# A new order, new engines and new buffer slots for a planned one-core kernel, and single loads in place of split ones

## The chip, the cores and the metric

The kernel runs on one core of a Trainium2 chip. The metric is the device time of one execution in microseconds (us), the median of several runs. The engines are called as in the profile: PE (TensorE, matmuls; PEld are its weight loads), DVE (VectorE), ACT (ScalarE), POOL (GpSimd) and SP (SyncE, which here issues every DMA).

## The reference

Gated linear attention with a state for each of 4 batches and 8 heads, and behind it a token mixer of low rank and an MLP, whose output is added:

```python
q, k, v, alpha: (4, 8, 768, 48) float32
for t in range(S):
    state = alpha[:, :, t, :, None] * state + einsum('bhd,bhe->bhde', k[:, :, t], v[:, :, t])
    y[:, :, t] = einsum('bhd,bhde->bhe', q[:, :, t], state)
x  = y as (4, 768, 384)
u  = x + (x.transpose(0, 2, 1) @ U @ V).transpose(0, 2, 1)      # U (768, 32), V (32, 768)
out = u + maximum(u @ w_ch1, 0) @ w_ch2                          # (384, 1536), (1536, 384)
```

## The kernel before, in words

The work of each batch goes through five stages. **Attention** works on units of a batch, written b.u here (0.4 is batch 0, unit 4). In batches 0 and 1 and the first two units of batch 2 a unit is half of the heads over two chunks of 64 pairs of tokens (`stage_pair`); the other units are one chunk of 128 tokens with all heads (`stage_gla`). A unit loads alpha, k, q and v (192 KB each, tiles `io`), takes the logarithm of alpha on ACT (tile `lt`, L390), sums it along the tokens on PE (L399 to L406), takes exponentials on ACT (tiles `ai`, `aa`, `tot`), multiplies k and q by them on POOL or DVE (tile `rkq`, L421), transposes the two products on PE (L449) and copies them out of PSUM on ACT or DVE (tile `kqt`, L294 or L296). Scores are matmuls of 64x64 tiles in pair units (L480) and of 64-row tiles in the others (L658); DVE masks them (L491, L668). The state's update is 64-row matmuls (L514) and, in batch 0, an identity matmul that adds the state before (L506), which must wait for DVE's state product (L529); in batch 1 DVE adds it instead (tile `sm`, L543). The output is full matmuls with the state (L562) and 64-row ones with the masked scores (L572), copied to `xb`.

**Mix** (`stage_mix`) multiplies x by U (L750) and by V (L771), DVE adds the two into `ub` (L781, eight quarters), and u is transposed on PE (L819) in batches 0 and 1, by DMA transposes on SP (L805) in batches 2 and 3. Batch 3's k and q are transposed by DMA too (L642). **MLP 1** (`mlp1`) has 24 groups for each batch of three matmuls (L851), each evicted with a relu by ACT (L861) or DVE (L863). **MLP 2** (`mlp2`) has three groups of four matmuls (L880) for each of 6 chunks, then DVE adds u (L886) and SP stores (L889, L891). The last chunk of the last batch is made in two column parts (240 and 144).

Nothing of the order is left to the compiler. `Plan.add` collects 1065 operations in the order of the program with the buffers that each reads and writes. `Plan.run` then emits them in the order of the string `TABLE`: three characters for each, of which the first two are the operation's number in base 64 and the third its engine (P, A, D, G for POOL, S). `SLOTS` has a character for each of the 736 buffers, at the place where a buffer is first used: which slot of its pool (`io` has 40, PSUM 8 banks) it takes. Each engine works its own operations in this order, waiting for what they need. The costs in the `P.add` calls are those of the search outside the kernel that made the strings. A field `mode` marks the shape of the PE tiles: F full, H and R 64 rows, Q 64x64, and three shapes of the mixer with 32 rows or columns.

Loads of pair units are always one transfer. Loads of other units go through L359 to L367: for eight of them `SPLIT` names a row at which the 128 rows are divided between two transfers, issued one after the other.

## Time and profile before

| | |
|---|---|
| time, median of 3 runs | 159.99 us (159.78 to 160.29) |
| the profiled execution | 159.3 us, span 157.5 us |
| granted TensorE clock in the clock column | 1.000 |
| DMA | 31.68 MB, mean 201 GB/s |
| first PE matmul, first MLP-1 group, last PE matmul | start 3.97, start 30.84, end 154.58 us |

The span is the time from the first to the last instruction; the profiled execution takes 1.8 us more than that. PE's matmuls are pipelined, so their lengths overlap, and the time that a group costs is read from its start to the start of the next one. A wait is given as waiting engine, what it was about to do, the releaser, and then the total in us, how often, and the longest.

### The profile page before, as it was taken

Reading aid. Unit: us, or ns where it says so; the run is one execution under the profiler, and the core shown is the slowest. Engines: PE = TensorE matmul, PEld = TensorE weight load, DVE = VectorE, ACT = ScalarE, POOL = GpSimd, SP = SyncE. Lnnn points to the kernel's source line nnn. Section 1 sums busy time; section 2 is a strip of 40 time slices with the busy share of each in tenths; the row PEclk is TensorE's granted clock in tenths of the full one; section 3 lists DMA queues with packets and bytes.
Section 4 is the critical chain, followed back from the end, with each engine's and each line's share of the span. In section 5 each row is a group of like instructions: output and inputs, shape, how many; then the busy total and the mean of one; then the engine's idle time right before and its main releaser. Section 6 shows DMA issues by size and latency. Waiting matters only on the chain.

```text
span 157.5 us, 4982 instructions
## 1 busy us (share of the span) xinstructions
PE 147.0 (93%) x1940; PEld 98.8 (63%) x1940; DVE 111.0 (70%) x253; ACT 85.7 (54%) x223; POOL 62.6 (40%) x103
## 2 busy tenths in 40 slices
PE   0499999889999999999999999999999999999992
PEld 0387676656687757666666765666667565666572
DVE  5168899956999636668899979399889634462351
ACT  4487998759897565499296740344552301532000
POOL 8155867635999704524375640055531000000000
PEclk9999999999999999999999999999999999999999
DMA  5999998999999979999989792899885062367475
GB/s 130 273 272 320 280 232 232 299 314 332 331 325 284 273 153 244 190 218 201 197 170 227 145 200 51 138 201 162 165 176 126 0 104 52 126 154 219 138 216 175
DMA packets 91275, 31.68 MB, mean 201 GB/s; under 512 B 84948, under 2 KB 91220, under 8 KB 91252
## 3 DMA queue, kind: packets, MB, share of 16 engines
q1 hardware_dynamic: 91252, 31.37, 83.4%
q8 instruction: 15, 0.25, 0.7%
q14 instruction: 8, 0.07, 0.1%
HBM read 23.89 MB, written 4.72 MB: 182 GB/s over the span
## 4 chain that ended last, share of the span: by engine, by line
PE 76%; SPq 17%; DMA 3%; issue 1%; DVE 1%; DVEq 0%
PE ps L880 31%; PE ps L851 29%; SPq L353 13%; DMA io<-in_k_dram 3%; PE ps L449 2%; SPq L326 2%; PE ps L658 2%; PE ps L572 1%; PE ps L480 1%; PE ps L725 1%; PE ps L630 1%; SPq L301 1%; PE ps L720 1%; PE ps L595 1%; PE ps L771 1%
## 5 line engine op out<-in xcount | busy, mean ns | idle before, releaser
L851 PE MATMUL ps<-uT,w_sb 128*128 128x384 bf16 x288 | 53.3, 326 | 0.7 <-DVE sm L543 0.4
L880 PE MATMUL ps<-w_sb,h1t 128*128 128x384 bf16 (+2 forms) x300 | 53.3, 320 | 0.0
L861 ACT ACTIVATE h1t<-ps 128x384 bf16<-128x384 f32 x54 | 25.3, 497 | 29.9 <-PE ps L851 28.0
L851 PEld LDWEIGHTS <-w_sb 128*128 128x128 bf16 x288 | 26.8, 98 | 16.9 <-issue 1.0
L880 PEld LDWEIGHTS <-h1t 128*128 128x128 bf16 x300 | 26.9, 98 | 15.4
L863 DVE TENSOR_SCALAR h1t<-ps 128x384 bf16<-128x384 f32 x42 | 22.2, 552 | 11.7 <-PE ps L851 11.6
L886 DVE TENSOR_TENSOR io<-ub,ps 128x384 f32<-128x384 bf16 (+2 forms) x25 | 13.1, 534 | 9.1 <-PE ps L880 8.8
L491 DVE TENSOR_TENSOR pm<-ps,maskp 128x512 bf16<-128x512 f32 x28 | 18.1, 682 | 0.1
L781 DVE TENSOR_TENSOR ub<-xb,ps 128x288 bf16<-128x288 bf16 x32 | 12.3, 448 | 4.9 <-ACT lt L390 3.1
L294 ACT COPY kqt<-ps 128x512 bf16<-128x512 bf16 x24 | 13.8, 592 | 3.2 <-PE ps L630 2.4
L668 DVE TENSOR_TENSOR pm<-ps,maskc 128x512 bf16<-128x512 f32 x20 | 12.7, 683 | 1.1 <-PE ps L658 1.1
L421 POOL TENSOR_TENSOR rkq<-io,aa 128x384 bf16<-128x384 f32 x12 | 10.9, 911 | 5.2 <-DMA io<-in_q_dram 4.2
L294 ACT CAST xb<-ps 128x192 bf16<-128x192 f32 (+1 forms) x24 | 8.1, 369 | 8.9 <-PE ps L725 6.5
L449 PE MATMUL ps<-ident,rkq 128*128 128x128 bf16 x112 | 11.1, 236 | 2.0 <-DVE rkq L421 1.5
L616 POOL TENSOR_TENSOR rkq<-io,aa 128x384 bf16<-128x384 f32 x9 | 8.5, 949 | 11.2 <-DVE io L886 8.0
L421 POOL TENSOR_TENSOR rkq<-io,ai 128x384 bf16<-128x384 f32 x8 | 8.1, 1015 | 11.6 <-ACT ai L413 11.6
L298 POOL CAST rv<-io 128x384 bf16<-128x384 f32 x19 | 10.0, 530 | 5.4 <-DMA io<-in_v_dram 4.8
L298 POOL CAST w_sb<-io 128x384 bf16<-128x384 f32 x17 | 8.2, 506 | 5.1 <-DMA io<-in_moe_w_ch_dram 5.1
L449 PEld LDWEIGHTS <-rkq 128*128 128x128 bf16 x112 | 7.7, 104 | 4.0 <-DVE rkq L421 1.7
L399 PE MATMUL ps<-lt,upto 128*128 128x384 bf16 x14 | 5.4, 385 | 4.8 <-ACT lt L390 4.8
L616 POOL TENSOR_TENSOR rkq<-io,ai 128x384 bf16<-128x384 f32 x5 | 4.6, 915 | 9.8 <-DMA io<-in_k_dram 5.0
L390 ACT ACTIVATE lt<-io 128x384 bf16<-128x384 f32 x14 | 7.2, 533 | 2.2 <-DMA io<-in_alpha_dram 2.2
(108 smaller groups left out, 208.7 us busy)
## 6 DMA issues: line engine op xcount, KB each, us to landing
...
```

Source lines behind the costliest of these rows:

```text
L294: nc.scalar.copy(dst, src)
L298: nc.gpsimd.tensor_copy(dst, src)
L353: lambda e: nc.sync.dma_start(t().rearrange("p (h j) d -> p h (j d)", j=2), src[b, hs, sl, :].rearrange("h (p j) d -> p h (j d)", j=2)),
L421: eng.tensor_tensor(jh(dst()[:, :, 0:D]), raw(a), jh(x()), op=ALU.mult)
L449: nc.tensor.matmul(dst, lhsT=ring()[:, HP * j + 2 * a : HP * j + 2 * a + 2, :].rearrange("t h w -> t (h w)"), rhs=ident, start=True, stop= ...
L491: nc.vector.tensor_tensor(dst, s2, maskp.to_broadcast([C, 2, 2, C]), op=ALU.mult)
L616: eng.tensor_tensor(dst()[:, :, 0:D], a(), x(), op=ALU.mult)
L851: nc.tensor.matmul(hb()[:, 0:TW], lhsT=w1_sb[:, ct, jt * 128 : (jt + 1) * 128], rhs=u_half(uT, ct, tt, b in QUEUE_U), start=(ct == 0), sto ...
L861: nc.scalar.activation(dst, hb()[:, 0:TW], AF.Relu)
L863: nc.vector.tensor_scalar_max(dst, hb()[:, 0:TW], 0.0)
L880: nc.tensor.matmul(hb()[:, 0 : hi - lo], lhsT=h1()[:, jt, c * C : (c + 1) * C], rhs=w2_sb[:, jt, lo:hi], start=(jt == 0 and not low), stop ...
L886: P.add({"DVE": 468}, lambda e, hb=hb, lo=lo, hi=hi: nc.vector.tensor_tensor(flat(ou)[:, lo:hi], (xb if low else ub)()[:, c, lo:hi], hb()[ ...
```

## The change

The two strings are replaced throughout; `Plan.run`, the operations and their matmuls stay. Decoded, the strings say this:

- Operations by engine: DVE 230 before and 233 after, ACT 222 and 227, POOL 88 and 80, PE 351 and SP 174 in both. Of the 96 MLP-1 evictions ACT has 54 before and 61 after, DVE 42 and 35. Of the 24 weight casts POOL has 17 before and 14 after, ACT 7 and 10.
- Neighbours on PE with a 64-row group next to a 64x64 group: 5 before, 8 after. All neighbours of unlike shape (H and R as one): 77 before, 76 after.
- PE's first seven groups and SP's first eight loads are the same. Then SP has v of 0.1 ahead of q of 0.1. PE's groups 8 to 15 were q transposes 0.1, state update 0.1, state update 0.0, k transposes 0.0, identity 0.1, identity 0.0, scores 0.1, scores 0.2; now they are state update 0.1, q transposes 0.1, identity 0.1, scores 0.2, state update 0.0, identity 0.0, k transposes 0.0, scores 0.1.
- The two small matmuls that spread V over the partitions stand behind batch 0's last output group before, and both ahead of it after; their copies (`ve_sb`) were one on DVE behind batch 0 and one on ACT, and are now one on DVE amid batch 0 and one on ACT. DVE's list between batch 0's last mask and the first `ub` sum was a state product, three `xb` copies, a `ve_sb` copy and a k copy; now it is one `xb` copy, a q copy and the mixer's small copy.
- Batch 0's MLP 1 began with groups mixed with the sums and transposes of 1.3, 1.1 and 1.2 (their k and q transposes came after 2 to 14 groups); now thirteen groups run before the transposes of 1.1. k of 1.1 was SP's 42nd operation and is now its 46th; its product with `ai` moves from DVE to POOL.
- In batch 3 the six DMA transposes of k and q have the order 2, 0, 1, 3, 4, 5 before and 0, 2, 1, 3, 4, 5 after. The loads of k and q of 3.4 stand behind batch 2's three DMA transposes of u in both; the scores of 3.4 come sooner after them on PE: they were the last but one of that batch's six and are now the fourth.
- PE's last groups were one of batch 3's chunk 4 and then five part-groups of chunk 3; now they are one of chunk 4 and two part-groups of chunk 3.

The diff, with the strings cut to their first and last lines:

```diff
 TABLE = """
-BASCzAC1PC4ABESDKADMPDPABISDOAC2ABBSBGSDRDDTPDjAA8SCcACePBFSC5GC7PDlPC3ADNADQDDSPC9DChAA9SCfACiDDVDBCSBDSC0AC6GC8PC+DDnA
...
-PQiDQjSQWPQaPQXPQYDQZSQbPQcPQdDQeS
+BASCzAC1PC4ABESDKADMPDPABISDOAC2ABBSBGSDRDDTPDjAA8SCcACePBFSC5GC7PDlPC3ADNADQDDSPC9DChAA9SCfABDSC0ABCSDoADnAA-
...
+PQlPQmPPnDPpDPdAQYDPtDQQPQaPQGPQRPQfPQLPQHPQnDQgPQIPQJDQMPQSPQTDQNPQhPQoSQKSNRSQODQUSQPSQiDQjSQZSQbPQcPQdDQeS
 """
 SLOTS = """
-AAAABBBBCAADEACCFADGBEFBBGACHCCBIJAHCAABAKBECLMNDBAOBDFACPCQDHAAEBGBBRBCSDCFTBUVDAWHCGAADXYZabDcdFECAADCDCeABEAGfgChijkl
...
-AGEDPHEQDJFBUcAd
+AAAABABBCAADEACAFBDABEFABBACGABAHDBIBAGJEEDFABACCAHIAGABHBABJAEBCKEFAHBBCGBCDFGABCFEBCAAHDLMNDCAAHBGJIGAAEBABBFDCAOPFQRS
...
+HFCDAQADGCEIXGIJ
 """
...
     PAIRS = {0: 3, 1: 3, 2: 1, 3: 0}
-    kn, qn, vn = (x.tensor.name for x in (k, q, v))
-    SPLIT = {
-        (2, 5, qn): 117, (2, 4, kn): 108, (3, 2, vn): 110, (3, 1, kn): 126,
-        (3, 2, qn): 117, (3, 0, qn): 108, (3, 0, kn): 110, (3, 3, kn): 126,
-    }
     QUEUE_T = tuple((3, c) for c in range(6))
...
-            at = SPLIT.get((b, c, src.tensor.name), C)
-            P.add(
-                {"SP": 1100.0},
-                lambda e: [
-                    nc.sync.dma_start(t()[lo:hi], src[b, :, c * C + lo : c * C + hi, :].rearrange("h t d -> t h d"))
-                    for lo, hi in ((0, at), (at, C)) if lo < hi
-                ],
-                w=[t],
-            )
+            sl = slice(c * C, (c + 1) * C)
+            P.add({"SP": 1100.0}, lambda e: nc.sync.dma_start(t(), src[b, :, sl, :].rearrange("h t d -> t h d")), w=[t])
```

More of the change, by code (lines that the diff above doesn't have):

```diff
@@ new lines @@
+SDUAC6DDCPA+SC8PBQSBMSBJSBHSCdGDDDDVACiDDEPDWPBKSDFDC+DBRSABSCgABLSDmACrPCsDDYDCtPCkPCuDCjGBSSETABNSBUSBOSBTSC-PDGPDZPD8
+ADBDDADCmAClPDpGDLGEVPCnAD+PDrPBPSEWAEYADXDBWSDaPCoPDtDDqGEXABYSAASBcSBkSAFGBVSBXSDHPDbDDkGEZGDcPDfPEaGDdDCpDDyPBgSAQSAM
+SDJADsPDePCqDEAAD-AEBADzPDgPAJPDuADiAD0DAKDDvPAOSDhADIAAgSD1PEcPD2DAiSAeSAWSAUSEeAASSBaSBdSEbPEiPBZSBeSBbSBfSDxDAaSECGCv
+PELPEEPGQAEGAEdDEDGEfPDwDEFPEHAGSPBmSAYSEUGEhDEgDBlSAcSD9GBhSGUACwPCxAEjPCyABoSGXGEMPEIPEkDEJDD3PBiSENDElPD4PEmPEnPEpAGT
+AEoAD5PGVABjSBqSEOPAkSADGGWGALGEPPEKDAoSAmSD6AD7AAGPEQPESDAqSERAGRGGZPGbDAHAEqPErDGnAHwAG+AEsPEwDExPGpPE1DEtDGYPHAPGrAGa
@@ new lines @@
+AHDAGsABpSARGEuDEvDE0DHyPEzDGfPANGAhGHXAE2PEyDGgDH1AE4PBnSHZPE6PGhDE3AAPABrSGcPAfGE5DGqAHzAATGGiDFAPAuSFBAAwSAySAsSA2SA0
+SHBAE7DA6SA4SAjAHCAGdDFUPE8PFVDGeDE9AE+PBzSFWPFYPFSPFQPFOPE-
+DAXAGuDGtGBsSHcAAVAFTAFXAFCPBxSBwSHEDFcPFePFDDHFDGoGFZAHbAHaAFdAFaPGwPFRDFmPG-GGvPFbAH0AHGPHHPFnAHIDFGPGyDGxAFoPAbGH3GHJ
+DFPDFfAAZGFHAAdGG2PHNPFpAHODGzPHdGB0SB4SBtSCASG3DG0DG4DHKPFEPFqPFFAIHACGSBuSBySFiPHPGH2DFjAFrAFgPIJPFhAG1DHLDHfPH5PH4PFI
+PHYAIKAHMDHeGG5GH7DILACBSB6SHQDIMAFJAGjPHgPFkPH6DHSPAlGHTPFlAHhDHiDHmPHUPGkPHVAHnDHWAB8SGlAH8PIOGHoDHjPAnAApAArGINGHpDIQ
@@ new lines @@
+PFKPFMPFLAISAGmAH9DGKPHrPCFSHkDHxGH+DHlDHsPCSSB1SIPPIRDFNAG6PG7PHRDHtPIIAG8AH-
+PIWPHuAIADITPHqGHvAIXDICPG9DIUDF+PF4PIVDIYGAvGIBGFsPB2SB3SAxGIDPAtAAzAIaPA3AA5AIZPIbPIcDKbAIEPGLPIFDA7GA1GIdDIGDF-PIePB-
+SB7SFtPIfDIgPGAPIjDGMPBvSIiDIkDFuPGBDF5PIhDIlPKEAFyPF6PIoDImDKdPKGPKJAKyAInDIpDKfAKHAF7DIsPGEPFvDIuPKIAGFPGGPFzPB9SItDLI
+AKKDKeALyAKLDCESB5SIvAACSB+SCQSKgAKiGGNDL0PIqPKkPF0PKhGKNPKmDIrDKjPL2AFwSGHDF1DKPDJKPKcGK0PK3AKlAI2PJQPL1AJWPKnPK1AK2ALK
+PLNAK4AL3GJLDLOAK6GI3DJMPCMSCDSCCSCTSK5GCYSGCSKoDCPSJNDJaPJYPJIPLMALLAJXAJbAK8PJcPKMPJJAJdAI6PJZDLeGK7PKOAI0PIwPKFGJRAKp
@@ new lines @@
+DK9AIxAK+DCLSKTPK-
+PI7DI1DKqPLJGLQGLdAKzGKUDKQPJSPLADCNSCISKSDJTAKrDKsDI4PJUPJVACXSCHSLfPJGPJOPLCPI5ANhAKVDLBDKtDLPDLhALEDI+PKWGI-ALDDLlDKR
+DNjPJCPJHALRPJEPLFGLTDJAPJPDJePLSPNnANkALgALiAJfDJFDLYPLkDJBAJDALjALUAI8PLZDKuPLGPI9AKvPLHAKxDKwAOWALVPLmPLWDL5PLnPKXPJ4
+PL4GL7DLtPLpAL6PLaGLoAIyPJ5PAEGAIGLXDLqPNmALzGOEALuDKYPCOSL8DIzANlACbSCUSCaSNyAL9PLvGL-
+DLrDJmPJnPJoPOGPLbPLsDKaDLcAN0PL+DLwPJ6POIAMAPCJSJ+PKZDLxDMBANzAN3AMCPOoAOJAOHAOKAJpDJ7DMDDJ-
+PCKSMEPJsPKAPMIDMHDMGDMJPO6AMFDMMDMNDNoGNiGNpGNqSCZSCRSJtPMOSJgPOpGOXAOFAN2AN1AN4AMKDOYPO8PNuPKBDOcAOZAMLDObAMPSJyPN5GN-
@@ new lines @@
+PNvDOLDO+AOMDONSOADJhPJzPOqPMQSCVSOtAOuAOaAORPJuPCWSOBGN6GJ0PJiPMbPMZPJ1DMdPOSDOrAOsAMcDJvDN7SMaAMeANrPOOPOQDNtDOdDJjDMT
+PNsDMVPMRPM1POeGMWAO9AM2DOPDM3POvGMvPMhPMUDGOSMwDOTDNwPJxSMSANxAOfSOwGMfPOUPOVDOjPMnPMoAMXPMpPM5PMiDOkDM4DMrPOxSMqAMYAMz
+PN8PMsDN+DOyPJ8SF9SM6AO0DN9DOgPGJSOzDM0APAGO-GMgAM-PNAAOlGM9PMtPO1PMjPO2DM+DOiDO3GGDSJkSPBSGPSF8SM7POCPO4PMxPMkAOhDMlPPC
+PMyDJ3SF2SO7AODAOmPPDDNHPO5ANBPPEDOnAMuAPFPNSPPGAMmAPHPNTPPIDM8DPJPNIPNJPJwSPKDPNDPMDNXPPLDPOPNYPPQDPRDPTSNNPNOPPPDNcPNd
+PF3SPSDNCPNZPNUPPUSNDPNePPWPPVSFxSNfDNEDNVDNKDNaDPuPPcPNPPJlSPkPPlDPgPPhAPYPP+PNQDQCPNGSJ9SGISP2PJ2SPwPQDAPvDP6PP7DPxAPX
```

37 lines of the change are left out of this document (6 added, 31 removed).

## The prediction

> **What bounds the kernel now.** I read the page's busy line, then the busy time by stretches of 4 us (columns: stretch, its length, then busy us of PE, weight loads, DVE, ACT, POOL; granted clock, DMA share, GB/s), and then who waits for whom, for PE alone.
>
> ```profile
> PE 147.0 (93%) x1940; PEld 98.8 (63%) x1940; DVE 111.0 (70%) x253; ACT 85.7 (54%) x223; POOL 62.6 (40%) x103
> ```
>
> ```profile
> 4.00:8.00 4.00, 1.86 (x17) 1.34 (x17) 0.68 (x3) 2.04 (x7) 0.48 (x2) 1.00 1.04 274
> ...
> 16.00:20.00 4.00, 3.58 (x87) 2.71 (x86) 3.29 (x9) 3.72 (x10) 3.58 (x5) 1.00 1.06 277
> 20.00:24.00 4.00, 4.00 (x108) 3.10 (x105) 4.00 (x9) 3.80 (x11) 2.55 (x5) 1.00 0.84 214
> 24.00:28.00 4.00, 3.75 (x109) 2.69 (x106) 3.66 (x11) 3.27 (x10) 2.42 (x4) 1.00 0.96 258
> 28.00:32.00 4.00, 3.59 (x63) 2.81 (x64) 3.65 (x9) 3.14 (x7) 2.89 (x6) 1.00 1.01 290
> 32.00:36.00 4.00, 3.57 (x27) 2.13 (x26) 2.60 (x7) 2.28 (x8) 1.10 (x3) 1.00 1.05 322
> 36.00:40.00 4.00, 4.00 (x32) 2.52 (x30) 2.81 (x6) 3.44 (x10) 2.70 (x6) 1.00 1.09 335
> ...
> 148.00:152.00 4.00, 4.00 (x28) 2.54 (x26) 1.95 (x4) 0.00 (x0) 0.00 (x0) 1.00 0.63 161
> ```
>
> ```profile
> PE ps L399 <- ACT lt L390: 4.8, 3, 4.0
> ...
> PE ps L851 <- DVE sm L543: 0.4, 1, 0.4
> ```
>
> From 36 to 152 us all 29 rows (the first and the last are shown) have PE at 4.00 of 4.00: nothing can be saved there except PE's own work. What a new order can win lies before 36 us, where PE idles (the 4.8 us are mostly the wait for the first load) and where DVE is nearly full too (4.00 at 20 to 24), and in the last 3 us. The PE timeline says how (columns: start, length with the modelled end, line, count, idle before it):
>
> ```profile
> 7.94 0.61 PE L449 MATMUL ps<-ident,rkq 128*128 128x128 bf16 x4 [1.47 <-DVE rkq L421]
> ...
> 10.10 0.37 PE L401 MATMUL ps<-lt,upto 128*128 128x192 bf16 x1
> 10.26 0.21 PE L402 MATMUL ps<-offd,ident 128*128 128x8 bf16 x1
> ...
> 14.29 0.25 PE L400 MATMUL ps<-lt,below 128*128 128x192 bf16 x1
> 14.38 0.25 PE L401 MATMUL ps<-lt,upto 128*128 128x192 bf16 x1
> ...
> 14.90 0.34 PE L514 MATMUL ps<-rv,rkq 64*128 64x96 bf16 x8
> 15.08 0.36 PE L572 MATMUL ps<-rv,pm 64*128 64x48 bf16 x16
> ...
> 17.77 0.34 PE L514 MATMUL ps<-rv,rkq 64*128 64x96 bf16 x8
> 18.04 0.80 PE L480 MATMUL ps<-kqt 48*64 48x128 bf16 x32
> ...
> 24.71 0.37 PE L572 MATMUL ps<-rv,pm 64*128 64x48 bf16 x16
> ...
> 30.84 0.65 PE L851 MATMUL ps<-uT,w_sb 128*128 128x384 bf16 x3 [0.26 <-DVE uT L296]
> ...
> 32.48 1.81 PE L851 MATMUL ps<-uT,w_sb 128*128 128x384 bf16 x9
> 34.70 0.65 PE L851 MATMUL ps<-uT,w_sb 128*128 128x384 bf16 x3 [0.40 <-DVE sm L543]
> ...
> 130.99 7.48 PE L851 MATMUL ps<-uT,w_sb 128*128 128x384 bf16 x45
> 138.30 0.81 PE L880 MATMUL ps<-w_sb,h1t 128*128 128x384 bf16 x4
> ```
>
> Steps are read from start to start. A 192-column matmul takes 0.16 us at 10.10 and 0.09 at 14.29: PE runs at half pace until 14.29, though the clock column says 1.00 in every row. An MLP-1 group (three matmuls) takes (138.30 - 130.99) / 15 = 0.487 us, so the three groups from 32.48 to 34.70 lost 2.22 - 1.46 = 0.76 us. The first MLP-1 group starts at 30.84; from there the kernel is PE's list plus those 0.76 us and little else.
>
> **The change part by part.** Each of the 351 PE groups runs in both tables with the same matmuls.
>
> *Changes of tile shape.* Eight 64-row matmuls (L514) take 15.08 - 14.90 = 0.18 us where 64-row work follows, and 18.04 - 17.77 = 0.27 where 64x64 work does: a change costs about 0.09, and a few ns more behind it. Adjacent groups of 64-row and of 64x64 tiles meet 5 times in the old order and 8 times in the new one, so the new charge has not made them fewer; the new order instead groups those stages, away from full tiles. All changes of shape together are 77 before and 76 after. That is one change: -0.1 us.
>
> *The start, to the first MLP-1 group.* Here I follow DVE, the fuller partner, in both orders.
>
> ```profile
> 13.75 1.89 DVE L491 TENSOR_TENSOR pm<-ps,maskp 128x512 bf16<-128x512 f32 x3
> ...
> 22.91 1.29 DVE L491 TENSOR_TENSOR pm<-ps,maskp 128x512 bf16<-128x512 f32 x2
> 24.12 0.35 DVE L529 TENSOR_TENSOR st<-ps,tot 128x192 bf16<-128x192 f32 x1
> 24.54 1.01 DVE L296 CAST xb<-ps 128x192 bf16<-128x192 f32 x3
> 25.46 0.55 DVE L296 CAST ve_sb<-ps 128x384 bf16<-128x384 f32 x1
> ...
> 26.64 3.01 DVE L781 TENSOR_TENSOR ub<-xb,ps 128x288 bf16<-128x288 bf16 x8
> ...
> 33.82 0.56 DVE L421 TENSOR_TENSOR rkq<-io,ai 128x384 bf16<-128x384 f32 x1 [0.71 <-DMA io<-in_k_dram]
> 34.30 0.35 DVE L543 TENSOR_TENSOR sm<-ps,st 128x192 f32<-128x192 f32 x1
> ```
>
> The first eight loads and PE's first seven groups are the same. The new DVE list has about 0.8 us more work ahead of batch 0's last mask (a ve copy of 0.46 and one more 0.33 copy), but its first mask can go at about 13.3 instead of 13.75, and its order leaves fewer holes behind; stepping through it with the row durations (mask 0.60, state 0.27, copies 0.33) I get the last mask done at 24.2, as now. Behind it the new order has less: the old DVE list has a state product, three xb casts and a ve copy there before the first u sum at 26.64; the new one has the state product and one ve copy ahead of the mask, gives xb casts to ACT, and on PE both ve matmuls stand ahead of the last output group instead of behind it. That last group can start just behind the mask, at 24.3 instead of 24.71, and the same 1.93 us (26.64 - 24.71) behind it the first u sum goes at about 26.3. Eight sums at 0.365 and a state product with its sum (0.53, in place of a mask of 0.60) later, DVE copies the transposed u at about 29.9. PE still has a score group to run first, so its first MLP-1 group starts at about 30.85, as before, but with 0.23 us more of its list done: adding up the steps of the groups ahead of it gives 18.86 us in the new order and 18.63 in the old. So: -0.2 us. The bounds are wide, since each step waits on another engine: -0.8 if every hole of 14 to 30 us that I count closes, +0.5 if two holes like the 0.51 and 0.70 us that DVE now has before its L529 products come back.
>
> *The start of the MLP.* The 0.76 us were lost because DVE's queue stood behind the k tile of batch 1, unit 1 (0.71 us for the DMA), and a PSUM bank waited behind it. The new order runs thirteen MLP-1 groups, 13 x 0.487 = 6.3 us, before it needs that tile, gives the product to POOL, and loads w1 blocks in the order of use. DVE still has a product on a q tile there. I take -0.45, between 0 and -0.76.
>
> *From 36 us on.* Seven more MLP-1 evictions go to ACT, POOL loses eight operations; both lie beside PE. If a cover goes, a late eviction costs PE its own length, some 0.5 us; I take 0, with 0 to +0.3.
>
> *The loads.* A split load costs two issues on SP.
>
> ```profile
> 77.28 1.20 SPq L363 DMA_DIRECT2D io<-in_v_dram  x2
> ...
> 81.22 0.67 SPq L363 DMA_DIRECT2D io<-in_v_dram  x1
> ```
>
> Eight of them at 1.20 - 0.67 = 0.53 us free about 4 us of SP between 74 and 91 us. PE waits for nothing there, so this is worth 0; what comes earlier behind it are loads of batch 3, and their buffers set when they may start.
>
> *The end.*
>
> ```profile
> 153.13 2.22 SPq L891 DMA_DIRECT2D out_dram<-io  x4
> 154.12 0.41 DVE L886 TENSOR_TENSOR io<-ub,ps 128x240 f32<-128x240 bf16 x1 [0.52 <-PE ps L880]
> 154.69 0.30 DVE L886 TENSOR_TENSOR io<-ub,ps 128x144 f32<-128x144 bf16 x1 [0.17 <-PE ps L880]
> ```
>
> Now chunk 4 is finished five part-groups before the end and the last store leaves right behind the last sum. In the new order chunk 4's last group stands directly before the last two, so three sums and three stores come within about 1 us, and the last sum waits for the one before it: +0.2 us (0 to +0.3).
>
> Sum: -0.1 - 0.2 - 0.45 + 0 + 0 + 0.2 = -0.55 us. The profiled execution took 159.3 us with a span of 157.5; the span becomes about 156.95 and that execution 158.75. The median of the three runs shown, 159.99, lies 0.69 above the profiled one, so the median becomes 159.4. About 0.3% (0.48 us) is what a measurement of this kernel can tell from no change, so this stands just past that line, at 159.5.
>
> **The rivals.** *No change that can be measured, 159.9.* The start is a ring of PE, ACT, DVE and POOL; each row of 16 to 32 us has two of them above 3.5 of 4. If a hole closed on one engine opens on another, the start gains 0 and the MLP's start 0.2: -0.1 - 0.2 + 0.2 = -0.1. For it: DVE is at 4.00 in 20 to 24 and has more work ahead of the last mask. Against it: the work behind that mask is less.
>
> *The clock comes later, 161.3.* The half pace ended at 14.29, 6.35 us after the last gap of note (1.47 us before 7.94). Behind its first L514 group the old PE order has another such group and a transposition before the identity product (L506) that needs DVE's state; the new one has one transposition there and then 64x64 scores that need two copies from ACT, and so should idle about 1 us in pieces between 11.5 and 13.5. If that restarts whatever the 6.35 us were, half pace lasts to 19.8, 5.5 us more, in which PE does up to 2.75 us less; some 0.9 us of that falls into holes that it has anyway from 14 to 20 us: +1.85 on the forecast. It decides if the first full-pace step lies after 15 us. Against it: the pieces are short, none as long as the gap of 1.47.
> [...]
>
> *A late tile in batch 3, 160.8.* k and q of batch 3, unit 4 are issued on SP behind three transposes that wait for batch 2's u sums, and their own transpose behind two stores and two more transposes. By SP's steps it lands about 1.6 us before PE's turn. A slip above that stops PE for about what it slips; I price it at 1.4.
>
> *The change does not do what it says.* The count of changes (5 to 8) is such a case already; it is inside the forecast.
>
> **How the numbers follow.** Forecast 0.50 (its own range 158.5 to 159.5), no change 0.28, later clock 0.15, late tile 0.07. Faster by over 0.3% is the forecast, 0.50; within it, the second case, 0.28; slower, the other two, 0.22. The range starts at 158.5, where the start gains 0.8 and the MLP's start all of its 0.76 against +0.2 at the end, a little short of the sum of all the best ends (0.05 is left below), and reaches to 160.9 over the late tile; the late clock's 0.15 stays outside.
>
> **What would show it.** Right: first full-pace step near 14.3; first L851 group at 30.6 to 31.1; no wait of L851 for DVE's L543 near 34; PE at 4.00 in all rows from 36 to 152; a last store 0.2 us further behind PE's end. Wrong: half pace beyond 15 us, a first L851 group after 31.3, or any row after 36 us with PE below 3.9.

## The result: slower by 1.4%, and the profile after

The changed kernel takes 162.10 us (161.83 to 163.05), the kernel before 159.92 (159.78 to 160.29); the ratio is 1.0143 [1.0098, 1.0188]. The forecast was 159.4, with a range that ended at 160.9: both the sign and the range were wrong. The profiled execution took 162.05 us with a span of 160.2, where before's were 159.3 and 157.5. Line numbers are 11 lower in the profile after (MLP 1 is L840, the output sum L875) and 13 lower in the experiments with single loads (L838, L873). Runs over 1.5% above the fastest of their kernel count as disturbed: the ratios leave them out (four of the six in experiment 12, whose ratio rests on two), and the profiles of experiments 1, 7, 8, 15 and 16 are such and are not read.

The first reading is the split that the prediction used: to PE's first MLP-1 group, and from there to the end. Timeline of PE, after (start, length, instruction, in brackets the idle time before it and what ended it):

```profile
13.56 0.24 PE L495 MATMUL ps<-st,ident 128*128 128x192 bf16 x1 [0.52 <-DVE st L518]
13.64 0.38 PE L438 MATMUL ps<-ident,rkq 128*128 128x128 bf16 x4
...
26.81 0.44 PE L760 MATMUL ps<-utx,ve_sb 32*128 32x96 bf16 x24 [0.36 <-DVE utx L292]
27.75 0.34 PE L388 MATMUL ps<-lt,upto 128*128 128x384 bf16 x1 [0.50 <-DVE ub L770]
...
31.86 4.47 PE L840 MATMUL ps<-uT,w_sb 128*128 128x384 bf16 x26
...
48.38 0.81 PE L840 MATMUL ps<-uT,w_sb 128*128 128x384 bf16 x4 [0.18 <-DVE sm L532]
...
108.20 0.97 PE L840 MATMUL ps<-uT,w_sb 128*128 128x384 bf16 x5 [0.48 <-DVE io L875]
```

The first MLP-1 group starts at 31.86 instead of 30.84, +1.02; from there to the end it is 160.2 - 31.86 = 128.34 instead of 157.5 - 30.84 = 126.66, +1.68. Together that is the span's +2.7. The half pace at the start was over by 13.56 us (a 192-column matmul takes 0.16 us from start to start at 9.88 and 0.08 at 13.56), no later than before (14.29), so the rival of the later clock is not what this profile shows. Behind 31.86 the groups run without a gap to 36: the three groups that lost 0.76 us have lost 0.08.

A PSUM bank that is not yet emptied when PE's next group needs it is called a late bank below. The second reading is PE's busy time in slices of 4 us (slice, length, then PE, PEld, DVE, ACT and POOL busy, clock, DMA share, GB/s), after:

```profile
24.00:28.00 4.00, 2.99 (x107) 2.19 (x104) 2.96 (x9) 3.27 (x11) 2.27 (x5) 1.00 1.03 302
...
48.00:52.00 4.00, 3.82 (x83) 2.77 (x81) 3.90 (x10) 3.61 (x11) 1.52 (x3) 1.00 0.97 333
...
76.00:80.00 4.00, 3.86 (x52) 2.38 (x47) 3.69 (x9) 2.39 (x7) 0.51 (x1) 1.00 1.01 204
...
104.00:108.00 4.00, 3.72 (x35) 2.08 (x33) 3.44 (x6) 2.23 (x5) 1.46 (x2) 1.00 1.12 136
108.00:112.00 4.00, 3.80 (x43) 2.44 (x43) 4.00 (x9) 0.97 (x2) 2.65 (x3) 1.00 1.01 219
...
132.00:136.00 4.00, 3.91 (x25) 2.25 (x24) 3.24 (x7) 0.35 (x1) 0.00 (x0) 1.00 0.35 85
```

The prediction named "any row after 36 us with PE below 3.9" as a sign that it is wrong; four of these rows are below. Start-to-start steps of the groups, less the step that such a group has elsewhere, give the size of each loss: 0.34 us at 47.8, 0.18 at 65.9, 0.41 at 76 to 78, 0.64 at 107.1, 0.09 at 111.4, 0.26 at 132.6, 0.10 at 44.4, and some smaller. With the 0.08 at the start of the MLP they make 2.27 us behind the first MLP-1 group, where before has 0.93, of which 0.76 lay at the start of the MLP.

What is late at 107? Timelines of DVE and POOL, after, and of DVE in experiment 11, which is the same kernel run again:

```profile
105.24 1.29 DVE L657 TENSOR_TENSOR pm<-ps,maskc 128x512 bf16<-128x512 f32 x2 [0.56 <-PE ps L647]
106.45 1.23 DVE L605 TENSOR_TENSOR rkq<-io,ai 128x384 bf16<-128x384 f32 x1
107.61 0.54 DVE L875 TENSOR_TENSOR io<-ub,ps 128x384 f32<-128x384 bf16 x1
```

```profile
106.35 0.92 POOL L605 TENSOR_TENSOR rkq<-io,ai 128x384 bf16<-128x384 f32 x1 [1.81 <-DMA io<-in_k_dram]
```

```profile
107.67 0.55 DVE L605 TENSOR_TENSOR rkq<-io,ai 128x384 bf16<-128x384 f32 x1
```

An output sum stands in DVE's queue behind two masks and a product, so the PSUM bank that it reads comes free at 108.15, and PE's L840 at 108.20 needs that bank. DVE is no bottleneck there (3.44 of 4); its order is, but not alone. The product ahead of the sum took 1.23 us, beside a product on POOL. In experiments 4 and 10 the two also overlap, and it takes 1.27 and 1.14 us; in experiments 2, 6, 11, 12 and 17 they do not, and it takes 0.55 each time. In experiments 2 and 11, which have after's order, nothing is lost at 104 to 112 us. So this loss comes when the two products meet; that the meeting is what lengthens DVE's product is read from these eight profiles and was not tested by an edit. The other losses look alike: at 47.8 the bank is held until DVE's batch-1 state sum (L532) has run, at 76 to 78 evictions stand behind DVE's masks and state sums. At 132 there is one more queue in the chain. DVE's and SP's timelines, after:

```profile
132.73 1.48 DVE L875 TENSOR_TENSOR io<-ub,ps 128x384 f32<-128x384 bf16 x3 [5.48 <-DMA out_dram<-io]
```

```profile
127.28 3.11 SPq L794 DMA_TRANSPOSE uT<-ub  x2
130.44 1.23 SPq L878 DMA_DIRECT2D out_dram<-io  x2
```

The sum waits 5.48 us for its `io` buffer, from which a store has to go first, and that store is issued only at 130.44, behind two transpositions of u.

The end, DVE's and SP's timelines after:

```profile
154.84 2.10 DVE L875 TENSOR_TENSOR io<-ub,ps 128x384 f32<-128x384 bf16 x4 [0.75 <-PE ps L869]
```

```profile
154.13 3.95 SPq L880 DMA_DIRECT2D out_dram<-io  x7
```

PE's last matmul ends at 156.61 and the span 3.6 us later (before: 154.58, and 2.9). Seven stores stand in one run on SP, and the last one starts 1.05 us behind PE's end instead of 0.44: +0.69 for the tail.

So the rest's +1.68 us is -0.33 (the steps of the groups behind the first MLP-1 group, 0.23 of which have moved ahead of it), -0.68 at the start of the MLP (0.76 to 0.08), +2.02 of other late banks (0.17 to 2.19) and +0.69 at the end; the sum is 1.70, and the 0.02 are rounding.

### The profile page after: what moved, and what is told of

Read it like the earlier page. It is cut to its first block, busy times and chain, and to the rows that moved or that the text cites. A ratio compares the mean times of both kernels' runs of the same rounds, so it can differ in the third digit from the quotient of the medians.

```text
span 160.2 us, 4952 instructions
## 1 busy us (share of the span) xinstructions
PE 147.8 (92%) x1940; PEld 98.0 (61%) x1940; DVE 110.5 (69%) x256; ACT 86.9 (54%) x228; POOL 57.7 (36%) x95
## 4 chain that ended last, share of the span: by engine, by line
PE 75%; SPq 7%; DMA 6%; DVE 4%; issue 2%; POOL 2%; ACT 0%; DVEq 0%; POOLq 0%
PE ps L840 28%; PE ps L869 26%; DMA io<-in_q_dram 5%; SPq L349 5%; PE ps L438 2%; PE ps L561 2%; SPq L794 2%; PE ps L469 2%; PE ps L647 2%; PE ps L808 2%; POOL rkq L410 2%; DMA out_dram<-io 1%; DVE ub L770 1%; PE ps L551 1%; PE ps L714 1%
## 5 line engine op out<-in xcount | busy, mean ns | idle before, releaser
L840 PE MATMUL ps<-uT,w_sb 128*128 128x384 bf16 x288 | 52.5, 326 | 0.9 <-DVE io L875 0.5
L869 PE MATMUL ps<-w_sb,h1t 128*128 128x384 bf16 (+2 forms) x300 | 51.5, 320 | 0.0
L850 ACT ACTIVATE h1t<-ps 128x384 bf16<-128x384 f32 x61 | 27.9, 497 | 27.4 <-PE ps L840 26.9
L840 PEld LDWEIGHTS <-w_sb 128*128 128x128 bf16 x288 | 26.6, 97 | 17.6 <-issue 1.8
L852 DVE TENSOR_SCALAR h1t<-ps 128x384 bf16<-128x384 f32 x35 | 18.7, 549 | 8.4 <-PE ps L840 8.2
L875 DVE TENSOR_TENSOR io<-ub,ps 128x384 f32<-128x384 bf16 (+2 forms) x25 | 12.7, 531 | 14.4 <-PE ps L869 6.0
L410 POOL TENSOR_TENSOR rkq<-io,aa 128x384 bf16<-128x384 f32 x9 | 8.5, 946 | 13.0 <-ACT aa L403 12.2
L410 POOL TENSOR_TENSOR rkq<-io,ai 128x384 bf16<-128x384 f32 x9 | 8.3, 923 | 7.5 <-ACT ai L402 4.1
L290 ACT COPY kqt<-ps 128x512 bf16<-128x512 bf16 x17 | 9.8, 590 | 2.0 <-PE ps L438 1.7
L294 POOL CAST rv<-io 128x384 bf16<-128x384 f32 x17 | 8.4, 504 | 4.7 <-DMA io<-in_v_dram 3.8
L681 POOL TENSOR_TENSOR st<-sm,tot 128x384 bf16<-128x384 f32 x6 | 5.2, 870 | 11.8 <-DVE sm L697 11.6
L605 POOL TENSOR_TENSOR rkq<-io,ai 128x384 bf16<-128x384 f32 x6 | 5.5, 913 | 9.6 <-ACT ai L594 7.8
L292 DVE COPY kqt<-ps 128x512 bf16<-128x512 bf16 x19 | 7.5, 413 | 1.8 <-PE ps L438 1.7
L294 POOL CAST w_sb<-io 128x384 bf16<-128x384 f32 x14 | 7.3, 528 | 4.2 <-DMA io<-in_moe_w_ch_dram 4.1
```

Of the source, the lines that this page charges most:

```text
L290: nc.scalar.copy(dst, src)
L294: nc.gpsimd.tensor_copy(dst, src)
L410: eng.tensor_tensor(jh(dst()[:, :, 0:D]), raw(a), jh(x()), op=ALU.mult)
L840: nc.tensor.matmul(hb()[:, 0:TW], lhsT=w1_sb[:, ct, jt * 128 : (jt + 1) * 128], rhs=u_half(uT, ct, tt, b in QUEUE_U), start=(ct == 0), sto ...
L850: nc.scalar.activation(dst, hb()[:, 0:TW], AF.Relu)
L852: nc.vector.tensor_scalar_max(dst, hb()[:, 0:TW], 0.0)
```

## The experiments

The theory after this reading: the order puts evictions behind other work on DVE, PE waits for their banks, and the start and the end cost the remainder (theory A, where an expectation gives letters). Rivals: the single loads, and tiles of batch 3 that come late because loads and transpositions now stand later on SP (theory C). Edits are told as changes of the decoded order; line numbers in them are before's, and "3.4" is unit 4 of batch 3.

### 1. Single loads in before's order

```diff
 TABLE, SLOTS: before's
-SPLIT, two transfers for eight of the loads
+one transfer for each load
```

> The order and slots of before, with every load a single transfer. Main theory (the new order and slots make the loss): as before, 159.9 us within 0.5, no new wait of PE in 60 to 110 us, since PE waited for no load of batch 2 or 3. Rival (the single loads make it: a load that takes one issue lands later or its neighbours collide): about 162 us, with PE below 4.00 in the rows from 60 to 110 us.

Ratio 0.9979 [0.9935, 1.0024]. The loads by themselves cost nothing that can be measured. The whole loss is that of the new order with its slots.

### 2. The new order with split loads

```diff
 TABLE, SLOTS: after's
+SPLIT, two transfers for eight of the loads
```

> The order and slots of after, with the eight loads split in two again. Main theory: as after, 162.1 us within 0.5, with the same late PSUM banks (0.64 us near 107 us, 0.34 near 48 us). Rival (single loads): back to about 160 us.

Ratio 1.0148 [1.011, 1.0185], as after. Its profile loses nothing to speak of near 107 us, where DVE's product takes 0.55 us; PE stops elsewhere. PE's timeline in this run (MLP lines are 1 lower than before's):

```profile
114.36 0.62 PE L657 MATMUL ps<-kqt 48*128 48x128 bf16 x16 [1.17 <-DMA kqt<-rkq]
```

The transposed k and q of 3.4 are 1.17 us late for their scores. That is the prediction's rival "a late tile in batch 3", at the tile it named; in the first profile after the tile was there 1.37 us ahead. The first MLP-1 group came at 31.54, and from there it was 128.96.

### 3. Before's order up to the first MLP-1 group, after's behind it

```diff
 every engine: before's operations up to PE's first MLP-1 group, then after's list without those
+34 buffers in other slots, as the seam needs
```

> The order of before up to its first MLP-1 group, the order of after for all that is left; 34 buffers get another slot, since the two slot lists do not fit together. Main theory (start, late banks and tail are three separate losses): the first PE group of MLP-1 starts near 30.9 us of before's scale instead of 31.9, the two later losses stay, and the time is 161.3 us (160.7 to 161.8). Rival (the losses are one ring, and what the start gains the engines give back as later waits): 162.1 us, with more PE idle after 36 us than the 2.4 us of after. If the first MLP-1 group starts near 30.9 and the time is near 160, the late banks too came from the start.

Ratio 1.0323 [1.0294, 1.0352]. The seam itself made losses: PE's rows from 32 to 40 us have 3.60 and 3.50 of 4, those from 44 to 52 us 2.81 and 3.16. The waits of PE show why:

```profile
PE ps L838 <- POOL w_sb L292: 1.2, 1, 1.2
```

Blocks of w1 that the new order loads early are late in this mixture. It tells nothing of the parts that it mixes. Inconclusive.

### 4. Five operations moved

```diff
 DVE near 107 us
+output sum of batch 1, chunk 0 (L886)
 second mask of 3.2 and first mask of 3.0 (L668), product of k of 3.3 (L616)
-output sum of batch 1, chunk 0 (L886)
 SP near 127 us
+second store of batch 0, chunk 0 (L889)
 transpositions of batch 3's u (L805) x2
-second store of batch 0, chunk 0 (L889)
 SP at the end: first store of batch 3, chunk 3, ahead of that of chunk 4
 PE near 13 us: scores of 0.1 two groups sooner, state update of 0.0 one sooner
```

> After, with five instructions moved on their own queue and nothing else: on PE the pair state group at 12.55 ahead of the scores at 11.98, and the scores at 13.96 ahead of the identity product that waited for DVE at 13.56; on DVE the output sum at 107.61 (L875) ahead of the two masks and the product of 1.2 us in front of it; on SP the store at 130.44 ahead of the two transposes of u in front of it; and the last store but one leaves ahead of the store that waits for the last sum. Main theory (a bank or buffer was held by an instruction that stood behind others on its own queue): -0.35 to -0.7 at the start, -0.5 to -0.64 at 107, -0.15 to -0.26 at 133, -0.3 at the end: 160.6 us (160.2 to 161.0). Rival (DVE is simply full there, and each move makes another bank as late): 161.7 to 162.3 us, with a PE idle of about 0.5 us still in the row from 104 to 112 us.

Ratio 1.0134 [1.0085, 1.0183]: no gain beside 1.0143. Slices of the profile, and DVE's sum near 132 us:

```profile
104.00:108.00 4.00, 4.00 (x38) 2.36 (x37) 3.83 (x7) 2.19 (x5) 1.83 (x2) 1.00 1.28 156
108.00:112.00 4.00, 4.00 (x45) 2.54 (x44) 4.00 (x9) 1.01 (x3) 2.95 (x3) 1.00 0.78 161
```

```profile
132.34 2.41 DVE L873 TENSOR_TENSOR io<-ub,ps 128x384 f32<-128x384 bf16 x5 [5.06 <-PE ps L867]
```

With the sum three places sooner 3.72 and 3.80 become 4.00 and 4.00, although DVE's product is long in this run too (1.27 us); near 132 the sum waits for PE and no longer for the store, and the row is 4.00. So the place in the queue is shown as a cause of these two losses. But the rows from 48 to 52 and from 76 to 80, near which nothing was moved, are 4.00 as well: some losses go with the time at which PE arrives. In this run half pace lasted to about 17.1 us, so the first MLP-1 group came at 32.90, and the rest took 127.10, 1.24 less than after; how much of that is the edit's is open. What the rest gained was lost at the start.

### 5. Before once more

```diff
 no edit
```

> The kernel before, unchanged, for a second look at its start: the end of PE's half pace has lain at 12.0, 13.3, 13.4, 14.2, 14.4 and 17.1 us in the six profiles so far. If that time belongs to the order, it is 14.2 to 14.5 here, and the first MLP-1 group starts at 30.8. If it floats from run to run, it is anywhere from 12 to 17, and the first MLP-1 group with it, 30 to 32 us.

159.66 us, span 157.9, first MLP-1 group at 31.15, rest 126.75: before's order repeats its two parts (30.84 and 126.66).

### 6. Other PSUM banks, order unchanged

```diff
 SLOTS: at five groups, from there on two PSUM banks change names
-at 44.7, 48.4, 66.2, 108.2, 112.0 us: a bank whose eviction stands late in a queue
+one that is free sooner
```

> After with the same order on every engine and with five PSUM banks exchanged, so that the late groups near 44.7, 48.4, 66.2, 108.2 and 112.0 us take a bank that was free earlier in the trace of after (44.07, 47.85, 61.69, 107.13 and 111.59 us). Theory A (the fault is the assignment of banks): the five losses of 0.10, 0.34, 0.18, 0.64 and 0.09 us go, 160.8 us. Theory B (at 105 to 112 us DVE itself is behind, standing behind masks and a product of 1.2 us, and any bank comes late): the loss near 107 stays at about 0.5 us in all, spread over the groups behind; only those at 48 and 66 go, 161.5 to 161.8 us.

Ratio 1.0224 [1.0152, 1.0297], no better than after (1.0143, and 1.0234 in experiment 11). Slices of its profile:

```profile
104.00:108.00 4.00, 4.00 (x38) 2.36 (x37) 3.10 (x7) 1.86 (x5) 0.91 (x1) 1.00 0.94 184
108.00:112.00 4.00, 4.00 (x46) 2.65 (x45) 4.00 (x8) 1.34 (x3) 2.36 (x3) 1.00 1.02 137
112.00:116.00 4.00, 3.28 (x39) 1.80 (x38) 3.48 (x8) 2.13 (x5) 2.27 (x3) 1.00 0.89 181
```

and a line of its waits of PE:

```profile
PE ps L645 <- DMA kqt<-rkq: 0.6, 1, 0.6
```

The rows from 104 to 112 are full, but that does not show the banks to be the cause: DVE's product takes 0.55 us in this run, and in experiments 2 and 11, with after's banks, the rows are full too. PE then waits up to 114.93 for the transposed tile of 3.4, which costs 0.80 us, and from 44 to 52 the losses have only moved (the slice 48 to 52 has 3.79). From here on theory C is tested beside A.

### 7. and 10. Late repairs

```diff
 as 4, but PE's order near 13 us as after, and
 SP at the end: first store of batch 3, chunk 3, five places sooner
 two MLP-1 evictions of batch 2 near 110 us
-DVE (L863)
+ACT (L861)
 DVE near 110 us: a state sum of 3.2 (L708) behind the copy of 3.2's output (L296)
 SLOTS: other banks for three groups (44, 48 and 66 us)
```

> After, changed from 44 us on only: the output sum of 107.61 ahead of two masks and a product on DVE; two MLP-1 copies of 108.7 and 111.8 from DVE to ACT (ACT is busy 0.97 of 4 us there); one product of 0.78 us behind a copy; the store of 130.44 ahead of two transposes of u; the chunk-3 store of 157.11 five places ahead; and the banks of three groups (44.7, 48.4, 66.2). Theory B: the loss after 36 us falls from 2.4 to 0.5 us, and the tail behind PE's last matmul from 2.7 to 2.2 us: 159.7 us (159.2 to 160.3), no longer slower than before, although the start is untouched. Rival (the order from 36 us on is too tight as a whole, and other banks come late instead): 161 us or more.

> The late repairs a second time, since its first profile had PE at half clock from 18 to 36 us. In that profile the loss after the first MLP-1 group was 0.76 us (2.27 in after) and the tail 2.21 (2.72). Theory C: the same two figures within 0.2 us, or a wait of up to 1.3 us for the transposed tile of batch 3, unit 4; its undisturbed time 0.7 to 2.0 us below after, run beside it. Rival: as after.

Ratios 1.0165 [1.0075, 1.0255] and, for the same kernel again, 1.0178 [1.0083, 1.0274]. The profile of the second:

```profile
28.00:32.00 4.00, 2.99 (x71) 2.37 (x71) 3.40 (x11) 2.86 (x9) 3.02 (x7) 0.78 0.97 319
...
104.00:108.00 4.00, 4.00 (x38) 2.37 (x36) 2.50 (x5) 2.38 (x6) 2.21 (x3) 1.00 0.84 162
```

Nearly all late banks are gone (only the row from 76 to 80, 3.86 in both, is as it was): the loss behind the first MLP-1 group falls from 2.27 to 0.75 us, the time from PE's end to the end of the last store's issue from 1.47 us to 0.95 (before: 0.77), the rest to 126.33, below before's 126.66. By theory A that leaves the later start, 1.02 us, less what the rest is shorter than before's, 0.33: 0.7 us or 0.4% above before. The time is 1.8% above, with 0.8% as the near end of its interval: half pace lasted beyond 19 us and came back at 30 to 33 (clock 0.78 and 0.80), and the first MLP-1 group started at 35.17. A start 3.3 us later than after's (35.17 less 31.86) leaves the loads behind it up to that much more time by my estimate, so this rest does not show what the repaired order does behind a start in time. Beside the unchanged kernel run on the same chip (experiment 11, 1.0234) the time is 0.6% lower, with intervals that overlap.

### 8. Late repairs, and the tile of 3.4 sooner

```diff
 as 7, and on SP
+transpositions of 3.3 and 3.4 (L642)
 two stores (L889)
-transpositions of 3.3 and 3.4 (L642)
 PE: scores of 3.3 (L658) ahead of those of 3.4, which come one group later
```

> The late repairs, with two output stores that stand on SP between the transposes of batch 3's units 1 and 3 moved behind the transposes of units 3 and 4, and the scores of unit 4 one group later on PE. In two of the six profiles with the new order (with split loads, and with the other banks) PE waited 1.32 and 0.80 us at 113 to 114 us for the transposed k and q of batch 3, unit 4; in the others that tile landed 0.1 to 1.4 us ahead of its use, in the two of before's order 3.9 us ahead. Theory C (with the late banks repaired PE comes to that tile earlier, and now the tile is what is late): the wait goes, and the time is 159.7 to 160.5 us, 1.6 to 2.3 below after. Rival (the banks were all of it and the other times of the late repairs came from the start): the same time as the late repairs, run beside it.

Ratio 1.0223 [1.0139, 1.0306]. One tile made sooner brings nothing in the time beside experiment 10's 1.0178; no profile shows whether the wait for it went.

### 9. and 13. Before's order improved

```diff
 9: before's order with single loads
 PE: sums of 0.3, scores of 0.4, q transposes of 1.1 and a part-group of chunk 3, each a few places sooner
 DVE: k product of 0.3, state product of 0.1, state sum of 1.0, each a few places sooner
 ACT: two exponentials, of 0.2 and 1.0, sooner
```

```diff
 13: before's order with single loads
 copy of the mixer's V part (ve_sb)
-ACT
+DVE, behind the copy of k of 1.0
```

> The order of before with single loads and nine small moves, most of them in its first 35 us: on PE one group of decay sums, one of scores, one transposition and one part of the last output chunk earlier; on DVE one product, one state and one sum earlier (the sum of 34.30 us ahead of the product that waits for its DMA); on ACT two decay copies earlier. Theory: what an order of this kernel costs is read from the instruction that a late PE group waits for; each of these was such an instruction, and the time falls by 0.5 to 1.1 us against before, 0.9930 to 0.9970 of it. Rival (the start is a ring, and other instructions come late): 0.9980 to 1.0020.

> Before with one instruction moved: the copy of the factored values that PE waits for at 26.2 us runs on DVE behind the k copy of batch 1, unit 0, as in after, instead of on ACT. Theory (DVE is the fuller partner at the start, and what the new order gives it there PE pays): the copy ends at about 26.9 instead of 26.2 us, the first MLP-1 group starts 0.5 to 0.7 us later, 0.3 to 0.45 % slower. Rival (the ring takes it up): no later than 0.2 us. If PE's longer idle stretch before 28 us is what lets the clock fall to half pace in 28 to 33 us, as in the second run of after, more of this kernel's runs than of before's show a mean clock below 0.992.

9: ratio 1.0005 [0.9967, 1.0044]; the gain is not there. Its profile has a rest of 125.94 us, 0.7 less than before's, since the loss at the start of the MLP is gone; but the first MLP-1 group came at 32.66. PE's timeline and slices of 2 us:

```profile
29.16 0.32 PE L386 MATMUL ps<-lt,upto 128*128 128x384 bf16 x1 [1.30 <-ACT lt L377]
```

```profile
28.00:30.00 2.00, 0.84 (x14) 0.76 (x13) 1.58 (x5) 1.42 (x3) 0.96 (x2) 0.95 0.98 264
30.00:32.00 2.00, 2.00 (x35) 1.50 (x33) 0.69 (x1) 1.62 (x4) 1.11 (x3) 0.50 0.96 293
```

An alpha load was late, PE stood for 1.30 us, and behind that its clock was halved (0.50 in the slice from 30 to 32). Whether that is typical of its runs or only of this one stays open: the time gives no gain, and 0.7 us would be 0.4%.

13: ratio 0.9977 [0.9938, 1.0015], no difference that can be told. It was a test of how the start answers to one copy:

```profile
26.44 0.31 PE L758 MATMUL ps<-utx,ve_sb 32*128 32x96 bf16 x12 [0.68 <-DVE utx L290]
```

PE waits 0.68 us for DVE here, and yet the first MLP-1 group starts at 31.05 and the rest takes 126.75, both as in before (30.84 and 126.66; 31.15 and 126.75 in experiment 5). This hole was taken up by the ring of engines before the MLP started; the expectation of a cost is rejected.

### 11. After once more

```diff
 no edit
```

> After, unchanged, on the chip of the other runs of this call. Loss after the first MLP-1 group 2.3 to 2.9 us, tail 2.7 us, first MLP-1 group at 31.5 to 32.0 us, 162.1 us within 0.6. If the losses at 107, 48 and 133 us are missing here, they were chance and no property of the order.

Ratio 1.0234 [1.0185, 1.0284], 163.04 us. First MLP-1 group at 33.20, rest 128.0. The losses at 48 (0.41), 66 (0.17), 76 to 78 (0.41) and 133 (0.40) are there again; the one at 107 is not, and PE waits at 114 for the transposed tile instead (0.39):

```profile
PE ps L647 <- DMA kqt<-rkq: 0.2, 1, 0.2
```

The start is late by the clock:

```profile
28.00:32.00 4.00, 4.00 (x49) 3.40 (x50) 3.17 (x9) 2.01 (x7) 1.49 (x3) 0.57 0.98 340
```

The slice 24 to 28 is as in the first profile after, 2.99 of 4; there the clock stayed at 1.00 behind it, here it fell to 0.57. The same kernel had 1.0143 on another chip: a difference of 0.9% between ratios taken on two chips is nothing yet. One chip each served experiments 1 to 4, 5 to 7, 8 to 11, 12 and 13, and 14 to 17.

### 12. Before's start and first 37 loads, then the repaired rest

```diff
 as 3, but behind the start the order of 7, with 8's two transpositions ahead of two stores;
 SP's first 37 operations are before's; an MLP-1 group and the sums of 1.3 stand two groups later on PE;
 599 buffers in other slots
```

> The start of before (its order on PE, DVE, ACT and GpSimd to the first MLP-1 group, its first 37 loads), and behind it the order of after with its late repairs: the sums, copies and stores of those kernels moved as there, the two stores behind batch 3's transposes, one MLP-1 group two places later. All slots are given anew, to the one that was free longest. Theory (what is slow in after is its start and single late instructions, not the order of the rest): first MLP-1 group at 30.8 to 31.2 us, loss behind it 0.3 to 0.8 us, tail 2.2 us, 159.2 us (158.6 to 160.0), 0.9930 to 1.0010 of before. Rival (the start of after is not at fault; the repaired rest is what keeps the runs of the late repairs at 161 to 163 us): 161 us or more.

Ratio 1.0276 [1.0193, 1.0359], from runs of 163.12 and 165.36 us; all six go up to 167.27. The first MLP-1 group starts at 30.99, as in before; the rest takes 130.31, four more than with the late start of experiment 10. PE's timeline:

```profile
120.66 0.40 PE L645 MATMUL ps<-kqt 48*128 48x128 bf16 x8 [2.33 <-DMA kqt<-rkq]
```

With the start given back, PE stops 2.33 us for the transposed tile of 3.5. This run speaks against theory A, by which it should have had before's time; by C the gain is lost at a tile. The profile is that of the fastest run, with a mean clock of 1.0. The other five have 0.988 to 0.990; the run profiled for experiment 14, in which half pace comes back, has 0.990 too, so a return of it probably adds to their times.

### 14. and 15. The tiles first, 16. and 17. only the stores behind

```diff
 14 (from 12) and 15 (from 7), on SP
+loads of k and q of 3.4
 third transposition of batch 2's u (L805)
-loads of k and q of 3.4
 transposition of 3.1 (L642)
+transposition of 3.5 (in 15 those of 3.3 and 3.4 too, which 12 and 14 have there)
 seven stores of batches 0 and 1 (L889)
-transposition of 3.5
```

```diff
 16 (from 12) and 17 (from 7): the same, without moving the two loads
```

> The kernel with before's start and the repaired rest, with moves on SP alone: the loads of q and k of batch 3, unit 4 ahead of the third transpose of u, and the seven output stores that stood between the transposes of batch 3's units 1 to 5 behind all of them. Theory C (in the new order the transposed tiles of batch 3 come with 0.05 to 1.6 us to spare where before has 1.5 to 4.0, and what the repaired banks win is lost there): the waits of 0.22 and 2.40 us at 113 and 118 us go, 159.0 to 160.2 us, and if a long idle stretch of PE is what brought the half pace into five of that kernel's six runs (mean clock 0.988 to 0.990), their clock is back at 0.997 to 1.0. Rival (the tiles are late for another reason, the loads and the transposes' own time): 162 us or more.

> The late repairs with the same moves on SP; its start is that of after. Theory C: from the first MLP-1 group to the end 125.3 to 125.6 us as in the two profiles of the late repairs, now in all runs, and 160.0 to 160.9 us (the start costs 0.4 to 1.0 us more than before's). Rival: 161.5 to 163 us as the late repairs.

> As the kernel with before's start and the repaired rest, and only the seven output stores on SP moved behind the transposes of batch 3's units 1 to 5; the loads of unit 4 stay behind the third transpose of u, which came 2.35 us late when they went ahead of it. Theory C: no wait for that transpose of u, 0.05 to 0.3 us for unit 4's tile, none for unit 5's; loss behind the first MLP-1 group 1.2 to 2.0 us, 159.7 to 160.7 us. Rival (the rest has other late tiles in most runs): 162 us or more.

> The late repairs with the same seven stores behind the transposes. Theory C: loss behind the first MLP-1 group 0.7 to 1.0 us and no wait for unit 4's or 5's tile of batch 3; 160.2 to 161.3 us, 0.8 to 1.9 us below after. Rival: 162 us or more.

14: ratio 1.0278 [1.0223, 1.0333]. 15: runs from 160.41 to 164.94 us, no ratio that can be given. In the profile of 14 the tiles of batch 3 are in time, and the u transposition that now stands behind the two loads is not. Timeline of PE and a slice of 2 us of experiment 14, whose clock is halved for a while behind the stop (0.63, then 0.52 in the slice from 112 to 114):

```profile
109.22 2.81 PE L838 MATMUL ps<-uT,w_sb 128*128 128x384 bf16 x12 [2.19 <-DMA uT<-ub]
```

```profile
110.00:112.00 2.00, 2.00 (x13) 1.05 (x11) 0.56 (x1) 0.80 (x2) 0.71 (x1) 0.63 0.94 188
```

16: ratio 1.0113 [1.0066, 1.016], against 1.0276 for 12: seven stores are out of the way of one transposition, that of 3.5 for which PE waited 2.33 us in 12. The two ratios are from two chips, and 12's from two runs, so their difference of 1.6% is no clean figure. Cleaner is the pair of 14 and 16, on one chip and apart only by the place of two loads on SP: 164.08 to 167.57 us with the loads ahead of the third u transposition, 161.43 to 162.61 with them behind it (one run of 364.28 aside). Two loads moved past one transposition cost 1.6%, the largest effect of one small edit here. 17: ratio 1.0123 [1.0069, 1.0177], first MLP-1 group at 31.73, rest 129.47. In its profile PE stops for no tile of batch 3 (that of 3.4 comes 0.05 us before its scores), and other loads are late. A line of ACT's waits:

```profile
ACT lt L575 <- DMA io<-in_alpha_dram: 4.7, 2, 3.3
```

ACT waits for an alpha load of batch 3 (4.7 us in two waits), and PE stands 0.69 us for ACT's tile at 92.6; similar stops at 44, 73 and 98 us cost about 0.4 to 0.6 each. No version is measurably faster than before.

## Why the prediction was wrong

**Tile shapes, -0.1: right.** PE's list of steps is 141.18 us against 141.29.

**The start, -0.2: wrong, +0.8.** The first MLP-1 group came at 31.86, +1.02 with 0.23 us more of the list done. The step that failed is the walk along DVE's list up to batch 0's last mask: "I get the last mask done at 24.2, as now". Before has DVE at 4.00 of 4 us from 20 to 24 us and its last mask done at 24.20 (the lines are in the prediction). DVE's timeline and the slice from 20 to 24 us, after:

```profile
23.60 0.69 DVE L480 TENSOR_TENSOR pm<-ps,maskp 128x512 bf16<-128x512 f32 x1 [0.23 <-ACT xb L290]
24.48 0.68 DVE L480 TENSOR_TENSOR pm<-ps,maskp 128x512 bf16<-128x512 f32 x1
27.24 3.00 DVE L770 TENSOR_TENSOR ub<-xb,ps 128x288 bf16<-128x288 bf16 x8 [0.48 <-ACT lt L379]
```

```profile
20.00:24.00 4.00, 3.82 (x102) 3.11 (x101) 3.67 (x8) 2.93 (x7) 2.89 (x5) 1.00 0.93 217
```

The first mask went at 13.43, nearly the 13.3 of the prediction, but the last one was done at 25.16 (24.83 in experiment 2, 24.86 in 6, 25.02 in 17): the new order leaves DVE more holes there, not fewer. Behind the last mask the prediction was right: 2.1 us to the first u sum, measured 2.08, and from there 4.55 us to the first MLP-1 group, measured 4.62. PE's stops of 0.36 and 0.50 us in that stretch, which make the slice 24 to 28 at 2.99, cost nothing beyond that, and experiment 13 shows a hole of 0.68 us to be taken up. In the new order without a return of half pace the group came at 31.5 to 31.9 (31.86, 31.54, 31.57, 31.73), so 0.7 to 1.0 us belong to the order, with the 0.23 of its list in them; the 32.9 to 35.2 of experiments 4, 10 and 11 come with half pace to about 17.1 us in 4, to about 19.9 and again at 30 to 33 in 10 (clock 0.78 and 0.80), and back at 28 to 32 in 11 (0.57).

**The clock: not in this profile.** Half pace was over by 13.56. With the same order of PE up to there it was over by 11.3 in experiments 2 and 11, by 12.2 in 6 and 17, and only at about 19.9 in 10, so it is no constant cost of the order, as the rival had it. That idle pieces of PE put off its end was the author's supposition; no run tests it. In before's start it was never later than 14.3 in the profiles read; whether the new order makes a late end more frequent is not settled.

**The start of the MLP, -0.45: right in kind.** It gave -0.68, near the better bound.

**From 36 us on, 0: the failed step.** "both lie beside PE. If a cover goes, a late eviction costs PE its own length, some 0.5 us; I take 0, with 0 to +0.3." Here it was +2.02. The cost of one was sized rightly (0.1 to 0.64 us); their number was never counted. I had looked at how many operations each engine has, and not at what stands ahead of each eviction in DVE's queue and which bank the next group takes; the order and the slots, which tell both, were there to read. That the place in the queue is a cause is shown by experiment 4 for the losses at 107 and 132 us; those at 48 and at 76 to 78 come and go with the time of the start, and no edit tests them by themselves.

**The loads, 0: right for the splits, wrong for what they stand for.** Experiment 1 bears out the 0. But the order of all loads changed with the search, and the prediction priced that at one tile. DMA in the slice from 88 to 96 us, before and after:

```profile
88.00:96.00 8.00, 8.00 (x141) 5.15 (x138) 6.63 (x15) 4.32 (x13) 2.92 (x4) 1.00 0.69 137
```

```profile
88.00:96.00 8.00, 8.00 (x144) 5.21 (x138) 5.79 (x13) 4.52 (x14) 2.83 (x5) 1.00 1.13 192
```

Before moves 137 GB/s there, after 192 (129 and 172 in the 8 us behind it): bytes that before has moved sooner are still coming. By the trace's DMA events the transposed tile of 3.4 landed 3.75 to 4.0 us before PE's scores of it in the profiles of before's order, and 0.05 to 1.37 us in those of the new one (14 aside, whose edit makes it 4.94), where 0.05 is what is left when PE waits for it. The prediction put the new order's margin at 1.6 us and gave the case 0.07; its margin was near the 1.37 of the first profile, and what it missed is how much less there is in other runs.

**The end, +0.2: too small, +0.69.** Only the sums were priced, not the run of seven stores ahead of the last one.

What ties these together is a row of pairs, the start of the first MLP-1 group and the rest of the span behind it:

| order | profile | first MLP-1 group | rest | span |
|---|---|---|---|---|
| before's | before, 5, 13 | 30.84, 31.15, 31.05 | 126.66, 126.75, 126.75 | 157.5, 157.9, 157.8 |
| before's | 9 | 32.66 | 125.94 | 158.6 |
| new, not repaired | after, 2, 11 | 31.86, 31.54, 33.20 | 128.34, 128.96, 128.0 | 160.2, 160.5, 161.2 |
| new, repaired | 4, 6, 17 | 32.90, 31.57, 31.73 | 127.10, 129.63, 129.47 | 160.0, 161.2, 161.2 |
| new, repaired | 12, 10 | 30.99, 35.17 | 130.31, 126.33 | 161.3, 161.5 |
| new, other edits | 3, 14 | 31.79, 31.51 | 131.5, 131.4 | 163.3, 162.9 |

In before's order the rest does not grow when the start is sooner: PE's list sets the end. In the new order the rest is mostly the longer the sooner the MLP starts, and in eight of the ten profiles the span lies at 160.0 to 161.5; in 3 and 14, where loads or a transposition came later by the edit, it is 163. That fits an end that is set by what SP brings, on its own time. It is a pattern in ten profiles and no proof: the spans of the runs without a profile go from 158.6 (experiment 15) to 165.8 us (14).

Shown are PE's waits for transposed tiles of batch 3 (experiments 2, 6, 11 and 12), for a transposed u (14) and, through ACT, for alpha (17), and by 14 against 16 that two loads moved on SP are worth 1.6%. That SP's whole queue, and no single load, is what takes the gain of the repairs is argued from this. A rival was not tested: the mean clock is below 0.992 in 22 of 46 runs of the kernels with repairs (6 to 8, 10, 12 and 14 to 17), in 9 of 75 runs of before taken beside the experiments and in 2 of 12 of after's order (after, 2 and 11). In the profiles of 9, 10, 11 and 14 a return of half pace lasts about 3.4 us by the clock column, in which PE does up to 1.7 us less by my estimate (half of 3.4), so part of what the repaired kernels failed to gain can be the clock. After's +1.4% is late banks, a later start and a longer end in its profile; where they were mended the time did not come back.

Left open: how the 1.1 to 1.2% of experiments 16 and 17 divide between the start and late loads, and why the 0.7 us that experiment 9's profile gains in the rest are not in its time. The section on the change says that before's scores of 3.4 were the last but one of batch 3's six; in the trace they are the last (118.79, with those of 3.5 at 118.56), which is part of why that tile has more time there.
